# The fourth product of the first layer in two levels, over all 1024 columns at once

## The chip, the core and the metric

The kernel runs on one core of one Trainium2 chip. Its time is the device time of one execution in microseconds, 1007.34 us as the median of three runs (1006.26 to 1007.73). TensorE (PE) multiplies; each matrix product is a weight load (PEld) and a pass. VectorE (DVE), ScalarE (ACT) and GpSimd (POOL) work element by element; SyncE (SP) issues the transfers. Each engine takes its instructions strictly in the order in which the program gives them to it, and waits on semaphores for the others.

## The reference

Attention without a softmax over pairs, its heads laid side by side as 512 columns, a two-dimensional Fourier transform of that, a normalisation and two dense layers. There are 8 batches of 576 tokens, 512 columns, 2048 hidden columns, all in float32.

```
q_s = softmax(q, over head_dim);  k_s = softmax(k, over seq)
x   = q_s @ (k_s^T @ v), heads side by side            # 8 x 576 x 512
u   = x + real(fft(fft(x, over seq), over columns))
un  = (u - mean(u)) / sqrt(var(u) + 1e-6)
out = u + max(un @ w_ch1, 0) @ w_ch2                   # 512 -> 2048 -> 512
```

## The kernel before

The tokens are treated in nine groups of 512 (the last tokens of the eight batches, 64 each, make a group of their own). The first group goes through plain dense layers (`plain`), while the weights are converted and combined. The other eight, called orders 1 to 8, use a fast scheme for 2 x 2 blocks with seven products instead of eight (`strassen`). While order n is in its dense layers, the attention of batch n + 1, its transform and its normalisation are worked in between, up to order 6; order 7 has the normalisation of the last group in it, and order 8 nothing.

**First layer, `up`.** Contraction, hidden columns and tokens are each halved: 256 of 512, 1024 of 2048, 256 of 512. Four blocks j, each with a tile of 128 hidden columns from both halves, go one after the other. In a block the products go in the order 1, 6, 5, 7, 2, 4, 3 (`ORDER`), each of them two pieces of 128 hidden columns by two of contraction by 256 tokens. A float32 matrix product is two passes in the trace, so a product is 8 passes of 256 columns (L1544). The seven products share three PSUM banks: 1 and 2 in `ba`, 6, 7 and 4 in `bb`, 5 and 3 in `bc`. What stands in a bank after the first product is read out, and the next is summed on top of it. So after product 1 ACT copies `s1` out of `ba` (L1515); after 6 DVE makes `u2` = bb + s1 and after 7 `u3` = bb + s1 (L1514); block (2,2) = bc + u3 follows at once, (2,1) = bb + s1 after product 4, (1,2) = bc + u2 after product 3 (all three L1555), and (1,1) is read from `ba` after product 2 by ACT (L1551). ACT puts a ReLU on the other three (L1556). When a block is whole, `a_side` (L405 to L408) makes the four sums which the second layer needs, in orders 2 to 6 on POOL, in 7 and 8 on DVE (`e`).

**Second layer, `down`.** Order 1 uses seven products of one level, and on the way `deepen` (L1579) makes the second combinations of the second layer's weights and stores them in `w2d` (L1585). Orders 2 to 8 (`deep_down`) use two levels: product 1 as a single one (L1641), the other six in pairs, `UNITS`, with seven products of 128 x 128 pieces each (L1671), with sums made by L1617. A pair gives each of its seven steps two products, which lie in the halves of one bank.

**Streaming.** The combined weights lie in DRAM: `w1s`, for each hidden tile seven slots of 256 columns, at places `WA_AT`; `w2s`; `w2d`. Four buffers of 1 MB in SBUF form a ring; `plan` is the list of all loads, chunk after chunk, `load(n)` issues chunk n on SP (L476), and `used(n)` issues chunk n + 4 when the products of chunk n are over. `gap(i)` are four spare places of 512 columns.

**Order of the work.** It is written out by hand. Each step has a nominal time, all steps are sorted by it, and are issued in that order, which sets the order on each engine. A nominal unit stands for two of the 256-column products by pieces; in an order the first layer has 56 units (`UP`), the second 50 (`TWICE`). Times named below count from the order's start. A product's end step comes half a unit before the product's nominal end, the ReLU 0.8 after its sum, the A side 0.8 after that. The attention of the next batch has its own times: maxima, subtractions on POOL (L804), transposes on DVE (L807) and exponentials on ACT (L817, pairs one unit apart) for four sets of queries, in orders 3 and 5 from 8.5, 14, 21.5 and 27.2 on, else from 6, 13.5, 21.5 and 27.2; the subtraction comes 0.9 after the maximum, the transpose 3.5 after it, the exponentials from 4.4 to 11.4 after it. Orders 3 and 5 also have the queries that two batches share, from 5 on, with a division at 9.8 (L946 to L957) and a transpose on TensorE at 13 (L985). The key products (L755) come at 7.3 and 17.3 (order 2: three units later), the query products (L840) at 28.5 or 29.

## Time and profile before

| | us |
|---|---|
| median of three runs | 1007.34 |
| lowest, highest run | 1006.26, 1007.73 |
| span of the profiled execution | 1006.6 |
| TensorE busy (modelled) | 995.6 |
| DVE, ACT, POOL busy | 718.6, 493.2, 442.9 |
| L1544, 256-column products of the first layer, three banks | 183.3 + 123.9 + 121.5 |
| L1641 and L1671 to bank bb (second layer) | 58.3, 103.8 |

The profiled execution's own time is known by its span from the first to the last instruction; it lies 0.7 us under the median and inside the spread of the runs. A group's line in the profile has line, engine, operation, out<-in, shapes and count, then the busy time and the mean of one in ns, then the idle time before them and what ended it. In a timeline the columns are the start, the length, engine, line, operation, out<-in, shapes and count, and in brackets the idle time of the engine before. Matrix products overlap: eight passes of 256 columns read 1.89 us long and start 1.73 us apart.

### The profile page before, as it was taken

The page shows a single profiled execution, that of the slowest core. Times are in us where ns is not written, and L with a number is a line of the kernel's source. Part 1 is how long each engine was busy: PE and PEld are TensorE (multiplying, and loading weights), DVE is VectorE, ACT ScalarE, POOL GpSimd, SP SyncE. Part 2 cuts the span into 40 slices and gives each one's busy share as a digit, 9 for nine tenths or more (in the row PEclk, how much of TensorE's full clock was granted, in tenths as well). Part 3 has the DMA queues.
Part 4 walks back from the last instruction along what each step waited for, and adds up shares of the span by engine and source line. Part 5 has one row for each costly group of instructions (what it writes and reads, how often), then busy time and mean ns, then how long its engine had stood idle before and what let it go on. Part 6 is the DMA issues. An engine that isn't in the chain of part 4 may idle for free.

```text
span 1006.6 us, 19808 instructions
## 1 busy us (share of the span) xinstructions
PE 995.6 (99%) x7562; PEld 855.7 (85%) x7562; DVE 718.6 (71%) x1356; ACT 493.2 (49%) x1277; POOL 442.9 (44%) x445
## 2 busy tenths in 40 slices
PE   8999999999999999999999999999999999999998
PEld 6844464888888899889988998899889998998897
DVE  6898898666765887588756877688667945685563
ACT  4585642872468228832775177625772342151200
POOL 4263420357535637664655465655646450040000
PEclk9999999999999999999999999999999999999999
DMA  9987499687989666975677577847753765674573
GB/s 300 258 281 245 158 240 346 205 243 226 342 283 272 230 230 219 266 237 210 251 220 242 206 269 237 253 174 270 231 204 135 267 213 200 224 265 172 183 256 132
DMA packets 123559, 236.37 MB, mean 235 GB/s; under 512 B 24184, under 2 KB 88440, under 8 KB 112840
## 3 DMA queue, kind: packets, MB, share of 16 engines
q1 hardware_dynamic: 123096, 234.58, 71.0%
q8 instruction: 60, 0.98, 0.4%
q14 instruction: 35, 0.29, 0.1%
q10 hardware_dynamic: 288, 0.26, 0.1%
q0 software_dynamic: 80, 0.26, 0.1%
HBM read 199.94 MB, written 39.06 MB: 237 GB/s over the span
## 4 chain that ended last, share of the span: by engine, by line
PE 87%; DVE 7%; ACT 3%; DMA 1%; issue 1%; SPq 0%; POOL 0%; DVEq 0%; POOLq 0%
PE bb L1544 16%; PE ba L1544 11%; PE bc L1544 11%; PE bb L1671 10%; PE ba L1671 7%; PE bc L1671 7%; PE bb L1641 5%; PE bc L1479 2%; PE bb L1760 2%; PE two L840 2%; PE one L755 2%; PE two L1207 1%; PE two L1264 1%; PE ba L1479 1%; PE bc L1760 1%; PE ba L1760 1%
## 5 line engine op out<-in xcount | busy, mean ns | idle before, releaser
L1544 PE MATMUL bb<-unT,big 128*128 128x256 f32 x768 | 183.3, 380 | 0.0
L1544 PEld LDWEIGHTS bb<-unT,big 128*128 128x128 f32 x768 | 144.8, 190 | 20.7 <-DVE u L1514 0.7
L1556 ACT ACTIVATE big<-big 128x512 f32<-128x512 f32 x96 | 59.8, 629 | 147.6 <-DVE big L1555 141.0
L1544 PE MATMUL ba<-unT,big 128*128 128x256 f32 x512 | 123.9, 382 | 0.0
L1544 PE MATMUL bc<-unT,big 128*128 128x256 f32 x512 | 121.5, 380 | 0.1
L817 ACT ACTIVATE qT<-q 32x128 f32<-32x128 f32 x384 | 117.9, 307 | 5.9 <-DVE q L807 0.8
L1544 PEld LDWEIGHTS bc<-unT,big 128*128 128x128 f32 x512 | 96.9, 190 | 13.7 <-DVE big L1555 0.5
L1544 PEld LDWEIGHTS ba<-unT,big 128*128 128x128 f32 x512 | 95.5, 190 | 13.9 <-issue 0.5
L1514 DVE TENSOR_TENSOR u<-bb,s 128x512 f32<-128x512 f32 x66 | 45.2, 685 | 85.0 <-PE bb L1544 66.5
L1671 PE MATMUL bb<-big 128*128 128x128 f32 x848 | 103.8, 276 | 0.2 <-DVE u L1678 0.2
L1671 PEld LDWEIGHTS bb<-big 128*128 128x128 f32 x848 | 98.9, 192 | 1.0 <-DVE u L1678 1.0
L1390 POOL COPY unT<-unT 32x256 f32<-32x256 f32 x98 | 42.0, 428 | 90.2 <-DVE unT L1382 85.9
L1621 POOL TENSOR_TENSOR x<-x,big 128x512 f32<-128x512 f32 x45 | 60.9, 1368 | 46.0 <-DVE big L1678 19.7
L1617 DVE TENSOR_TENSOR big<-big 128x512 f32<-128x512 f32 x98 | 79.9, 842 | 0.0
L1671 PE MATMUL ba<-big 128*128 128x128 f32 x640 | 79.0, 276 | 0.0
L1671 PEld LDWEIGHTS ba<-big 128*128 128x128 f32 x640 | 75.0, 192 | 0.8
L1390 ACT COPY unT<-unT 32x256 f32<-32x256 f32 x126 | 50.7, 402 | 31.3 <-DVE unT L1382 29.5
L804 POOL TENSOR_TENSOR q<-q,qm 128x512 f32<-128x512 f32 x24 | 25.8, 1073 | 88.2 <-DVE qm L799 53.1
L405 POOL TENSOR_TENSOR big<-big 128x512 f32<-128x512 f32 x24 | 30.4, 1268 | 68.4 <-ACT big L1556 68.4
L1641 PE MATMUL bb<-big 128*128 128x256 f32 x256 | 58.3, 379 | 0.0
L1555 DVE TENSOR_TENSOR big<-bc,u 128x512 f32<-128x512 f32 x64 | 44.0, 688 | 17.3 <-PE bc L1544 16.4
L1641 PEld LDWEIGHTS bb<-big 128*128 128x128 f32 x256 | 48.0, 190 | 6.1
(336 smaller groups left out, 1917.9 us busy)
## 6 DMA issues: line engine op xcount, KB each, us to landing
big<-w2d SPq DMA_DIRECT2D x67, 1024.0 KB, 4.6
big<-w1s SPq DMA_DIRECT2D x64, 896.0 KB, 4.7
big<-w2s SPq DMA_DIRECT2D x16, 1024.0 KB, 4.8
big<-in_w_dram SPq DMA_DIRECT2D x21, 512.0 KB, 6.0
w2d<-big SPq DMA_DIRECT2D x42, 256.0 KB, 6.5
kb<-in_kT_dram SPq DMA_DIRECT2D x28, 320.0 KB, 7.8
q<-in_q_dram SPq DMA_DIRECT2D x28, 256.0 KB, 6.0
vt<-in_v_dram SPq DMA_DIRECT2D x84, 80.0 KB, 2.7
```

The source lines that it names most:

```text
L405: e1.tensor_tensor(out=to(4), in0=at(2), in1=at(3), op=ALU.add)
L817: nc.scalar.activation(to[t, i * Q:i * Q + Q], one, ACT.Exp)
L1390: copy(to, of)
L1514: plus = lambda t: V.tensor_tensor(out=temp(t), in0=box["bb"][:], in1=box["s1"][:], op=ALU.add)
L1544: nc.tensor.matmul(bank()[:, i, :], lhsT=w[:, WA_AT[m], k * P:(k + 1) * P], rhs=self.unT[g][:, B_AT[m], k, :], start=first and i == 0 and ...
L1555: steps = [(0, lambda: V.tensor_tensor(out=hp(i), in0=bank()[:], in1=u()[:], op=ALU.add)), (0.8, lambda: nc.scalar.activation(hp(i), hp(i) ...
L1556: (0.8, lambda: nc.scalar.activation(hp(i), hp(i), ACT.Relu))]
L1617: e.tensor_tensor(out=to(o), in0=to(x), in1=to(y), op=op)
L1621: E.tensor_tensor(out=x, in0=x, in1=tile(m), op=ALU.add)
L1641: nc.tensor.matmul(box[name][:, i, :], lhsT=h[p][:, A_AT[m], i * P:(i + 1) * P], rhs=self.stream[n][:, p, :], start=p == 0 and (m != 1 or ...
L1671: nc.tensor.matmul(box[place[n]][:, i, :], lhsT=own(m)(A_AT[n])[:, f, :], rhs=w[:, r // 2, r % 2 * P:r % 2 * P + P], start=first and f == ...
L1760: nc.tensor.matmul(bank()[:, i, :], lhsT=h[p][:, A_AT[m], i * P:(i + 1) * P], rhs=w[:, p, :], start=first and i == 0 and p == 0, stop=p == ...
```

## The change

In orders 2 to 8 the fourth product leaves the four blocks of the first layer (`REST`), and is made once for all four, with a second level of the same scheme: its 256 x 1024 x 256 is halved in each direction, and seven products of four pieces of 128 x 128 by 128 tokens remain. This is `deep_up`, put between block 0 and block 1.

- Its weights' second combinations are made once, in order 1 at the start of the second layer (`deepen_up`): eight loads of slot `WA_AT[4]` into a buffer of the ring, two sums on DVE, two on POOL, seven stores to the new `w1d`. Slot 4 of `w1s` is now the last one, so that later loads take six slots.
- In each later order four of the seven weight sets come as a chunk of the ring, after the two chunks of block 0; the three others come by `weights` into `gap(1)` to `gap(3)`, at nominal 3.
- DVE makes four differences of 128 x 128 of the tokens (`minus`, nominal 8.0 to 8.9), into `gap(0)`. The seven products use the banks `ba`, `bb`, `bc` as before, 1.02 units apart, with a copy to `s1`, `u2`, `u3`, three more sums on DVE and one copy on ACT; the results go to slot `A_AT[5]` of the four blocks.
- In the blocks, `there` writes bb + s1 after product 7 straight to the place of (2,1), and (2,2) is made from it. `late` adds the deep result to (2,1), on `e` (POOL in orders 2 to 6, DVE in 7 and 8), and a ReLU follows. For block 0 that and the A side wait for the deep product: late add at 20.2, A side at 22.0.
- A first layer has now 4 x 12 + 7.2 = 55.2 units (`DEEP_UP`, `ups`).

```diff
-WA_AT = {1: 0, 2: 1, 3: 6, 4: 2, 5: 4, 6: 5, 7: 3}
+WA_AT = {1: 0, 2: 1, 3: 5, 4: 6, 5: 3, 6: 4, 7: 2}
+REST = tuple(m for m in ORDER if m != 4)
+DEEP_UP = 7.2
...
+        self.w1d = d.tile([P, len(ORDER), GT], F32, tag="w1d", name="w1d", bufs=1)
+        self.plan, self.at_up, self.at_down, self.at_deep = [], {}, {}, {}
         for at in range(1, B + 1):
-            self.base[at] = len(self.plan)
-            self.plan += [self.w1s[p][:].rearrange("p a n -> p (a n)") for pair in PAIRS for p in pair]
+            slots = len(ORDER) - (at > 1)
+            self.at_up[at] = []
+            for j, pair in enumerate(PAIRS):
+                for p in pair:
+                    self.at_up[at].append(len(self.plan))
+                    self.plan.append(self.w1s[p][:, 0:slots].rearrange("p a n -> p (a n)"))
+                if at > 1 and j == 0:
+                    self.at_deep[at] = len(self.plan)
+                    self.plan.append(self.w1d[:, 0:4].rearrange("p a n -> p (a n)"))
+            if at == 1:
+                self.at_deep[at] = len(self.plan)
+                self.plan.append([self.w1s[p][:, WA_AT[4]] for i in range(2) for p in [pair[i] for pair in PAIRS]])
+            self.at_down[at] = len(self.plan)
...
-    def strassen(self, product, step, out, early=lambda *a: []):
+    def strassen(self, product, step, out, early=lambda *a: [], u3=None):
...
+        if u3:
+            there = lambda: V.tensor_tensor(out=u3, in0=box["bb"][:], in1=box["s1"][:], op=ALU.add)
+            ends[7] = [(0, there)] + at(0.8, out[2, 2](get("bc"), lambda: u3) + out[2, 1](None, None))
...
-        for m in ORDER:
+        for m in REST if u3 else ORDER:
...
-                    if i == 2:
+                    if i == 2 and not wait:
                         steps.append((1.6, lambda: self.a_side(hp, hp, e, e)))
...
+            def late(t, hp=hp, relu=relu):
+                return [(t, lambda: e.tensor_tensor(out=hp(1), in0=hp(1), in1=hp(4), op=ALU.add)), (t + 1.6, lambda: relu(1))]
+
+            out = {(1, 1): c11, (2, 2): other(3), (1, 2): other(2)}
+            out[2, 1] = other(1) if not deep else lambda *_, j=j, late=late: late(1.6) if j else []
+            steps += at(t, self.strassen(product, 1, out, u3=hp(1) if deep else None))
+            t += 2 * len(REST if deep else ORDER)
+            waits = (-0.5, 2 if deep and j == 0 else 4.5 if j < NP // 2 - 1 else -0.5)
+            steps += [(t + dt, lambda n=n: self.used(n)) for dt, n in zip(waits, n)]
+            if deep and j == 0:
+                steps += at(t, self.deep_up(order, g))
+                t += DEEP_UP
+                steps += late(t + 1) + [(t + 2.8, lambda hp=hp: self.a_side(hp, hp, e, e))]
...
+    def deep_up(self, order, g):
...
+        place = {1: "ba", 2: "ba", 6: "bb", 7: "bb", 4: "bb", 5: "bc", 3: "bc"}
...
+        to = lambda i: self.hblock(A_AT[5], i % 2, 1 - i // 2)
...
+        def weights():
+            for i in range(3):
+                nc.sync.dma_start(self.gap(1 + i).rearrange("p j n -> p (j n)"), self.w1d[:, 4 + i, :])
...
+        def product(k):
...
+            for j in range(4):
+                w = self.stream[n][:, 2 * k + j // 2, j % 2 * P:j % 2 * P + P] if k < 4 else self.gap(k - 3)[:, j, :]
+                nc.tensor.matmul(box[name][:, j, :], lhsT=w, rhs=b_at(B_AT[m]), start=first and j == 0, stop=True,
+                                 skip_group_check=True)
+            if k == 3:
+                self.used(n)
...
+        def ends(m):
+            if m == 1:
+                nc.scalar.copy(temp("s1"), box["ba"][:])
+            if m == 6:
+                plus(temp("u2"), "bb", "s1")
+            if m == 7:
+                plus(temp("u3"), "bb", "s1")
+                plus(to(3), "bc", "u3")
+            if m == 2:
+                nc.scalar.copy(to(0), box["ba"][:])
+            if m == 4:
+                plus(to(2), "bb", "s1")
+            if m == 3:
+                plus(to(1), "bc", "u2")
+
+        steps = [(-9, weights)]
+        for i, (o, x, y) in enumerate(((4, 1, 0), (1, 3, 1), (5, 3, 4), (6, 2, 5))):
+            steps.append((-4 + 0.3 * i, lambda o=o, x=x, y=y: minus(o, x, y)))
+        for k, m in enumerate(ORDER):
+            steps += [(1.02 * k, lambda k=k: product(k)), (1.02 * k + 0.9, lambda m=m: ends(m))]
+        return steps
+
+    def deepen_up(self):
...
+        return [(0, lambda: make(V, 4, 2, 3, ALU.add)), (1, lambda: make(V, 2, 0, 2)), (1, lambda: make(G, 5, 4, 0)),
+                (2.5, lambda: make(G, 6, 1, 5)), (0, lambda: keep(raw)), (6, lambda: keep([m for m in ORDER if m not in raw])),
+                (7, lambda: self.used(n))]
```

More of the change, by code (lines that the diff above doesn't have):

```diff
@@ L439, in combine @@
             engines, times = (nc.vector,) * 4, (0, 0.4, 0.8, 1.2)
-            to, first, second = self.w1s[p][:], slice(0, 2), slice(2, 3)
+            to, first, second, third = self.w1s[p][:], slice(0, 2), slice(6, 7), 2
             one, two = halves(w[:, p, :]), quarter(3).unsqueeze(1)
@@ L475, in load @@
         w = self.big[:, k * NP * HD:(k + 1) * NP * HD]
-        self.nc.sync.dma_start(w[:, :self.plan[n].shape[1]], self.plan[n])
+        some = self.plan[n] if isinstance(self.plan[n], list) else [self.plan[n]]
+        end = 0
+        for of in some:
+            end += of.shape[1]
+            self.nc.sync.dma_start(w[:, end - of.shape[1]:end], of)
         self.stream[n] = w.rearrange("p (a n) -> p a n", n=HD)
@@ L1534, in up, with product @@
         nc, V = self.nc, self.nc.vector
-        steps = []
-        base, e = self.base[order], V if order >= B - 1 else nc.gpsimd
+        steps, t = [], 0
+        deep, e = order > 1, V if order >= B - 1 else nc.gpsimd
         for j in range(NP // 2):
             hp = lambda i, h=self.hpairs(j, 2): h[:, :, i, :]
-            def product(m, bank, first, j=j):
+            n = self.at_up[order][2 * j:2 * j + 2]
+            def product(m, bank, first, n=n):
                 def run(i):
-                    w = self.stream[base + 2 * j + i]
+                    w = self.stream[n[i]]
                     for k in range(2):
@@ L1862, in timed, with ups @@
         return steps + at(t + 24 + 1.65 * soon, blk.norm(groups[b]))
+    def ups(order):
+        return UP if order == 1 else 2 * len(REST) * (NP // 2) + DEEP_UP
     fetch, convert = blk.weights()
```

57 lines of the change are left out of this document (42 added, 15 removed).

## The prediction

> **What bounds the kernel now.** I read the page first, then stretches of one order each, then the timeline engine by engine around the first layer of orders 3, 4 and 8. The page (span; busy share; granted clock by slices; chain):
>
> ```profile
> span 1006.6 us, 19808 instructions
> PE 995.6 (99%) x7562; PEld 855.7 (85%) x7562; DVE 718.6 (71%) x1356; ACT 493.2 (49%) x1277; POOL 442.9 (44%) x445
> PEclk9999999999999999999999999999999999999999
> PE 87%; DVE 7%; ACT 3%; DMA 1%; issue 1%; SPq 0%; POOL 0%; DVEq 0%; POOLq 0%
> ```
>
> Order 4 by stretches: length, then busy time (instructions) of PE, weight load, DVE, ACT, POOL, clock, DMA share, GB/s:
>
> ```profile
> 496.60:602.70 106.10, 106.10 (x921) 97.76 (x921) 77.34 (x146) 58.92 (x163) 60.96 (x59) 1.00 0.71 232
> ```
>
> TensorE is never without work, and its clock is full. So each microsecond of TensorE that the change saves comes off the end, and each wait it adds goes on. The reader is to see that today nothing waits: the slack between dependent products is what the change spends. The profiled span, 1006.6, lies 0.7 below the median of the runs, 1007.34; I add my sum to the median.
>
> **What the products cost.** Timeline of order 4, first the 256-column products of L1544 (8 passes each), then the 128-column ones of the second layer (16 passes each):
>
> ```profile
> 516.94 1.89 PE L1544 MATMUL bb<-unT,big 128*128 128x256 f32 x8
> ...
> 523.85 1.03 PE L1544 MATMUL ba<-unT,big 128*128 128x256 f32 x4
> ...
> 469.84 1.95 PE L1671 MATMUL bc<-big,unT 128*128 128x128 f32 x16
> ...
> 480.56 1.95 PE L1671 MATMUL bb<-big 128*128 128x128 f32 x16
> ```
>
> Four products lie from 516.94 to 523.85: 1.73 us each. Six pieces lie from 469.84 to 480.56: 1.787 each, 0.112 a pass. Removed in an order: the fourth product of four blocks, 4 x 1.73 = 6.91 us. Added: seven products of 8 narrow passes, 56 x 0.112 = 6.25, or 0.89 each. Gain 0.66 an order, 4.6 over orders 2 to 8. That is all the change can win, and only without waits.
>
> **What an add costs TensorE.** Order 8, where the other engines have little else to do (PE, DVE, ACT), and two rows of order 7:
>
> ```profile
> 913.55 1.89 PE L1544 MATMUL bb<-unT,big 128*128 128x256 f32 x8
> 915.28 1.89 PE L1544 MATMUL ba<-unT,big 128*128 128x256 f32 x8
> 915.48 0.69 DVE L1514 TENSOR_TENSOR u<-bb,s 128x512 f32<-128x512 f32 x1 [0.78 <-PE bb L1544]
> 916.20 0.69 DVE L1555 TENSOR_TENSOR big<-bc,u 128x512 f32<-128x512 f32 x1
> 920.46 1.89 PE L1544 MATMUL ba<-unT,big 128*128 128x256 f32 x8
> 920.66 0.69 DVE L1555 TENSOR_TENSOR big<-bc,u 128x512 f32<-128x512 f32 x1 [1.03 <-PE bc L1544]
> 921.38 0.63 ACT L1556 ACTIVATE big<-big 128x512 f32<-128x512 f32 x1 [1.10 <-DVE big L1555]
> 922.44 0.59 ACT L1515 COPY s<-ba 128x512 f32<-128x512 f32 x1 [0.43 <-PE ba L1544]
> ...
> 831.58 0.68 DVE L1514 TENSOR_TENSOR u<-bb,s 128x512 f32<-128x512 f32 x1
> 832.32 1.99 PE L1544 MATMUL bb<-unT,big 128*128 128x256 f32 x8
> ```
>
> An add starts 0.20 after the next product and lasts 0.69; in order 7 an add ends at 832.26 and the waiting product starts at 832.32, 0.06 later. So a bank is free 0.95 after its product's end; with a second add behind (916.20 + 0.69, against 915.28) after 1.67.
>
> Ordinary blocks: the fourth product separated the seventh from the third, which reuses bank bc after u3 and (2,2). Now only the second does, 1.73 against 1.67: it fits by 0.06 when DVE is idle. In the first block of orders 7 and 8 one of the new differences (nominal 8.0) stands between the two adds. The small 128x128 form takes 0.28 (row below): 1.67 + 0.28 - 1.73 = 0.22 late. In the first block of the earlier orders an attention batch lies there and covers it.
>
> **The deep product, orders 7 and 8.** Its first product is copied to s1 by ACT, but the last ReLU of block 0 (12.3) is queued before that copy (12.9). Counting from the end of block 0 (920.46 stands for it): ReLU 921.38 to 922.01, copy to 922.62, u2 to 923.35, seventh product at 923.40 instead of 920.46 + 3 x 0.89 = 923.14. That is 0.26 late, and the fourth, which needs u3 out of bb, 0.05. Gain there: 0.66 - 0.31 - 0.22 = 0.13 an order.
>
> **The deep product, orders 2, 4, 6.** ACT is shared with the exponentials of the next batch (L817), pair by pair at one nominal unit. DVE, ACT and POOL of order 4:
>
> ```profile
> 506.79 1.89 PE L1544 MATMUL bb<-unT,big 128*128 128x256 f32 x8
> 508.52 1.89 PE L1544 MATMUL bc<-unT,big 128*128 128x256 f32 x8
> 507.55 1.25 ACT L817 ACTIVATE qT<-q 32x128 f32<-32x128 f32 x4
> 512.03 1.26 ACT L817 ACTIVATE qT<-q 32x128 f32<-32x128 f32 x4
> 513.31 0.59 ACT L1515 COPY s<-ba 128x512 f32<-128x512 f32 x1
> 511.81 1.04 POOL L804 TENSOR_TENSOR q<-q,qm 128x512 f32<-128x512 f32 x1 [3.56 <-DVE qm L799]
> 512.81 1.27 POOL L405 TENSOR_TENSOR big<-big 128x512 f32<-128x512 f32 x1
> 516.74 1.27 POOL L408 TENSOR_TENSOR big<-big 128x512 f32<-128x512 f32 x1
> 521.30 0.71 DVE L807 STREAM_TRANSPOSE q<-q 128x512 f32<-128x512 f32 x1 [0.56 <-POOL q L804]
> ```
>
> The third product moves to 506.79, the deep one starts at 508.52. Its copy stands behind the ReLU (509.44 to 510.07) and the pair of nominal 12.4 (0.63): 510.70 to 511.29. Then u2 to 512.02 and the seventh at 512.08, due at 511.20: 0.88 late, plus 0.05.
>
> **Orders 3 and 5** have the shared queries as well, and DVE is the later one. Order 3:
>
> ```profile
> 399.62 0.69 DVE L1555 TENSOR_TENSOR big<-bc,u 128x512 f32<-128x512 f32 x1
> 404.16 0.68 DVE L1555 TENSOR_TENSOR big<-bb,s 128x512 f32<-128x512 f32 x1
> 401.45 1.89 PE L1544 MATMUL bb<-unT,big 128*128 128x256 f32 x8
> 403.17 1.89 PE L1544 MATMUL bc<-unT,big 128*128 128x256 f32 x8
> 404.90 0.60 PE L985 MATMUL one<-ident,q 128*128 128x128 f32 x4
> 230.47 0.28 DVE L1129 TENSOR_TENSOR eo<-eo 128x128 f32<-128x128 f32 x1
> ```
>
> From 400.31 to 404.16 DVE serves attention, 3.85 us, then the add of the fourth product. In the new order the same work, with four differences of 0.28, stands before the add that frees bc: it ends at 405.98. The deep fifth product wants bc at 404.96. Behind it ReLU, copy and u2 follow (0.63, 0.59, 0.69 with releases): the seventh at 408.02, due at 406.29 with the transposes of L985 (0.44) counted. That is 1.73 late, plus 0.05.
>
> **The A side of block 0, orders 2 to 6.** Today POOL makes it at nominal 15.1, behind one subtraction of the queries (L804) and clear of the next (22.4). The change moves it to 22.0, behind the late add (20.2, 1.27 on POOL). Counted from the end of the deep product: last add to 0.89, late add to 2.2, four sums (512.81 to 518.01: 5.2) to 7.4, L804 to 8.45. The transpose L807 (nominal 25), which waited 0.56 at 521.30, now holds DVE until then and ends at 9.2. Behind it stand `there` (0.69), a maximum of the queries (0.68) and (2,2): 11.2. The third product of block 1 wants bc at 5 x 1.73 = 8.64 plus an attention batch of 1.8 (524.80 to 526.60 in the next fence, order 4): 10.44. So 0.75 late. The fence also has a stretch of order 1 and L1617 in two stretches, 350 to 388 and 960 to 1000 us, for what follows.
>
> ```profile
> 524.80 1.16 PE L840 MATMUL two<-pairs,qT 64*64 64x65 f32 x64
> ...
> 526.60 1.13 PE L1544 MATMUL ba<-unT,big 128*128 128x256 f32 x4
> 245.00:258.00 13.00, 13.00 (x71) 11.72 (x70) 8.39 (x21) 2.03 (x3) 4.94 (x5) 1.00 1.05 347
> L1617 DVE TENSOR_TENSOR big<-big 128x512 f32<-128x512 f32 x11 | 10.3, 962 | 0.0
> L1617 DVE TENSOR_TENSOR big<-big 128x512 f32<-128x512 f32 x10 | 6.4, 683 | 0.0
> ```
>
> **At nothing.** DVE gives up four adds (2.8 us) and gets five and four differences (4.6) an order, ACT two copies (1.2), POOL four late adds (5.1): beside TensorE, apart from the places above; without that cover the sum is 8 us an order. A late add also delays a ReLU and the sums for the second layer's units, which have the single product (L1641) and attention in front. Streaming: each of eight loads shrinks by 128 KB, 1 MB of kept weights and three loads of 256 KB come in, 0.75 MB more. The SP queue passes three more issues and one load in an order whose DMA share is 0.71. The ring's wait at the deep chunk is for the fourth deep product, well ahead.
>
> **Order 1's second layer.** deepen_up adds eight loads (1 MB) and seven stores (1.75 MB), four 128x512 sums and a held ring slot. The SP queue and the DMA engines are full there (245 to 258: share 1.05, 347 GB/s). Low end 0, since it only adds work and TensorE has weights ahead; high end 2.75 MB / 347 GB/s = 7.9 us. I take 0: TensorE is busy for all of that stretch, and the seventh product's weights are wanted some 25 us later.
>
> [...] L1617, two SBUF inputs, takes 962 ns beside POOL (350 to 388) and 683 without (960 to 1000): 0.28 an instruction. [...] The adds that free banks read PSUM and one SBUF tensor, so I book none of it.
>
> **Sum.** Orders 2, 4, 6: 0.66 - 0.93 - 0.75 = -1.0 each, -3.1. Orders 3, 5: 0.66 - 1.78 - 0.75 = -1.9 each, -3.7. Orders 7, 8: +0.3. Together 6.5 us slower: 1007.3 + 6.5 = 1013.8. The waits booked add up to 11.1 us (6.5 + 4.6): with half of them the kernel is 1 us slower, and with half as much again elsewhere (16.7 less 4.6) 12 us slower.
>
> **Rivals.** (1) Faster: the waits don't form, because queries and ReLUs drift ahead of TensorE while it waits once and later waits vanish. For: the copies of orders 7 and 8 start at once. Against: the queues are in order, and L817 already pushes the copy to 513.31 in order 4. Gain 4.6 less 0.1 an order: 1003.4. It decides when the waits of orders 2 to 6 stay below 0.73 us an order. (2) Cancelling at about that point: 1007.3. (3) The transfers of order 1 are not hidden: 1013.8 + 7.9 = 1021.7; for it the share of 1.05, against it that TensorE has none of the waits today. [...]
>
> **How the numbers follow.** Forecast 0.58, (1) 0.24, (2) 0.06, (3) 0.06, (4) 0.06. Two runs of this kernel differ by about 0.1%, so 0.2% is what can be told from no change. Faster 0.24, same 0.06, slower 0.70. The range goes from 1004 into (1) to 1021; the forecast's own is 1008.5 to 1020.
>
> **What would show it.** Right: in orders 2 to 6 TensorE idles before the seventh deep product (copy to s1 late) and before the third product of block 1 (DVE behind L807 behind POOL); orders 7 and 8 a little shorter; passes of 0.112. Wrong: in orders 2 to 6 TensorE goes through the deep product and block 1 in its own time (6.25 us, then 1.73 a product), or it waits for a load of weights in order 1 or 2.

## The result, and the profile after

The changed kernel takes 1066.4 us, the median of four runs (1065.0 to 1068.8), against 1006.9 for the kernel before beside it: a ratio of 1.059 (95% interval 1.058 to 1.061). It is 59.5 us slower. The prediction had said 1013.8, with a range from 1004 to 1021: the sign was right, the size was not.

The page of the changed kernel (span, busy shares, the chain that ended last):

```profile
span 1063.2 us, 20359 instructions
...
PE 1007.0 (95%) x7730; PEld 860.2 (81%) x7730; DVE 759.5 (71%) x1401; ACT 499.6 (47%) x1291; POOL 469.3 (44%) x467
...
PE 61%; DVE 23%; DMA 5%; ACT 4%; issue 3%; POOL 3%; SPq 1%; POOLq 0%; DVEq 0%; ACTq 0%
```

TensorE was the chain to 87% and is now 61%; DVE went from 7% to 23%. DVE's busy time rose by 41 us (718.6 to 759.5), while the sums that the change adds to it come to some 20 us at their undisturbed durations: 12.6 by the prediction's count (seven orders of 4.6 - 2.8), eight late adds of 0.69 in orders 7 and 8, and two sums of 0.7 in order 1. The rest is, on balance, instructions that became longer. The transform's thirty differences of 128 x 128 (L1129 before, L1147 after), which the change leaves as they are, went from 8.5 to 25.0 us.

Where the time lies is seen by cutting the trace at the first product of each first layer (L1544 before, L1566 after). Length of orders 1 to 7 in us (order 8 has no end of that kind; its time to the end of the span is 98.2 before and 98.3 after):

| order | 1 | 2 | 3 | 4 | 5 | 6 | 7 |
|---|---|---|---|---|---|---|---|
| before | 110.0 | 106.5 | 105.3 | 106.0 | 105.4 | 107.0 | 93.3 |
| after | 112.3 | 121.4 | 114.5 | 117.0 | 114.6 | 118.4 | 93.4 |
| more | 2.3 | 14.9 | 9.2 | 11.0 | 9.3 | 11.4 | 0.1 |

Orders 2 to 6 lose 55.8 us, order 1 loses 2.3, orders 7 and 8, with no attention in them, are as long as they were. Order 4 by stretches (length, then busy time of PE, weight load, DVE, ACT, POOL; clock; DMA share; GB/s), to be read beside the row of order 4 in the prediction:

```profile
521.40:638.40 117.00, 108.61 (x944) 99.08 (x943) 84.08 (x151) 59.99 (x165) 65.67 (x63) 0.99 0.69 218
```

In the kernel before, the view of TensorE's waits has no row at all for orders 2 to 6 (284 to 815 us). In the changed kernel the same view (tile and line that waited, engine and line that released it: us in total, times, longest), from 285 to 872 us:

```profile
PE two L1225 <- DVE eo L1148: 13.2, 5, 2.7
PE bb L1566 <- DVE u L1532: 11.3, 7, 2.1
PE bc L1566 <- DVE big L1580: 10.4, 9, 2.5
PE bb L1629 <- DVE u L1640: 5.1, 3, 2.2
PE ba L1566 <- POOL unT L1408: 2.2, 1, 2.2
PE one L1003 <- DVE q L975: 1.6, 2, 0.8
PE bc L1566 <- DVE x L1890: 0.8, 1, 0.8
PE two L858 <- DVE F L1043: 0.7, 1, 0.7
```

These are 45.3 us of idle time. Counted from the start of one product to the start of the next, the wait at 538.67 below comes to 2.34 us where its idle time is 2.18; where the text says how late a product is, it is by the starts. The deep product itself (L1629) has 5.1 of the 45.3. The largest, 13.2, is a wait of the transform (L1225), which the change doesn't touch; the next two, 21.7 together, are ordinary blocks (L1566) that wait for `u2` and for the sums that free `bc`. The longer waits of order 4 in the timeline (start, length, engine, line, out<-in, count; in brackets the idle time before):

```profile
538.67 1.16 PE L1629 MATMUL bb<-big 128*128 128x128 f32 x8 [2.18 <-DVE u L1640]
...
564.43 3.68 PE L1566 MATMUL bb<-unT,big 128*128 128x256 f32 x8 [2.11 <-DVE u L1532]
567.94 1.89 PE L1566 MATMUL ba<-unT,big 128*128 128x256 f32 x8
...
593.14 1.22 PE L1225 MATMUL two<-ft,eo 128*128 128x144 f32 x8 [2.65 <-DVE eo L1148]
```

The product at 564.43 waits for `u2`, and `u2` for the copy to `s1`. The block's first product starts at 556.98 and is over by 558.9, but its copy stands behind exponentials on ACT until 563.07:

```profile
561.15 1.89 ACT L835 ACTIVATE qT<-q 32x128 f32<-32x128 f32 x6
563.07 0.58 ACT L1533 COPY s<-ba 128x512 f32<-128x512 f32 x1
563.68 0.69 DVE L1532 TENSOR_TENSOR u<-bb,s 128x512 f32<-128x512 f32 x1 [4.18 <-ACT s L1533]
```

Five of the seven waits for `u2`, 9.1 of the 11.3 us, are of this kind; one of 1.8 in order 5 stands behind sums of the attention on DVE.

The product at 564.43 takes 3.51 us to the start of the next instead of 1.73. The stretch around it shows why (clock is the last number but two):

```profile
564.20:568.00 3.80, 3.57 (x9) 2.88 (x10) 3.77 (x4) 3.64 (x13) 3.72 (x3) 0.55 0.21 39
```

After the wait of 2.1 us TensorE had a clock of 0.50 for 3.4 us (564.5 to 567.9). There are four such stretches in the trace, all of 3.4 us at 0.50 (from 335.8, 359.7, 564.5 and 796.6 us), each behind one of the longer waits (2.48, 2.58, 2.11 and 2.13 us). By an estimate from their length, half of 3.4, each costs another 1.7 us or so, about 7 us in all. Waits of that length are not always followed by one: four of the five before L1225 (2.65 to 2.66 us) were not.

### The profile page after: what moved, and what is told of

Its sections match the earlier page's. It is cut to its first block, busy times and chain, and to the rows that moved or that the text cites. A ratio compares the mean times of both kernels' runs of the same rounds, so it can differ in the third digit from the quotient of the medians.

```text
span 1063.2 us, 20359 instructions
## 1 busy us (share of the span) xinstructions
PE 1007.0 (95%) x7730; PEld 860.2 (81%) x7730; DVE 759.5 (71%) x1401; ACT 499.6 (47%) x1291; POOL 469.3 (44%) x467
## 4 chain that ended last, share of the span: by engine, by line
PE 61%; DVE 23%; DMA 5%; ACT 4%; issue 3%; POOL 3%; SPq 1%; POOLq 0%; DVEq 0%; ACTq 0%
PE bb L1786 10%; PE bc L1566 7%; PE ba L1786 6%; PE bc L1786 6%; PE bb L1566 6%; PE ba L1566 6%; PE bb L1756 3%; DMA w2d<-big 2%; PE bc L1497 2%; DVE eo L1147 2%; PE bb L1629 2%; DVE big L1580 2%; DVE eo L1148 2%; PE ba L1497 1%; PE bb L1497 1%
## 5 line engine op out<-in xcount | busy, mean ns | idle before, releaser
L1566 PE MATMUL bb<-unT,big 128*128 128x256 f32 x544 | 133.6, 388 | 11.3 <-DVE u L1532 11.3
L1566 PE MATMUL bc<-unT,big 128*128 128x256 f32 x512 | 124.9, 387 | 11.3 <-DVE big L1580 10.4
L1566 PEld LDWEIGHTS bb<-unT,big 128*128 128x128 f32 x544 | 103.6, 193 | 29.6 <-DVE u L1532 14.8
L1566 PE MATMUL ba<-unT,big 128*128 128x256 f32 x512 | 122.8, 382 | 2.2 <-POOL unT L1408 2.2
L1566 PEld LDWEIGHTS bc<-unT,big 128*128 128x128 f32 x512 | 95.9, 191 | 29.8 <-DVE big L1580 16.3
L1566 PEld LDWEIGHTS ba<-unT,big 128*128 128x128 f32 x512 | 95.9, 191 | 16.4 <-POOL unT L1408 2.6
L1732 DVE TENSOR_TENSOR big<-big 128x512 f32<-128x512 f32 x98 | 75.6, 799 | 0.0
L1532 DVE TENSOR_TENSOR u<-bb,s 128x512 f32<-128x512 f32 x38 | 26.0, 685 | 42.0 <-ACT s L1533 20.8
L1793 DVE TENSOR_TENSOR u<-bb,s 128x256 f32<-128x256 f32 x40 | 16.8, 421 | 51.0 <-PE bb L1786 48.3
```

Of the source, the lines that this page charges most:

```text
L1532: plus = lambda t: V.tensor_tensor(out=temp(t), in0=box["bb"][:], in1=box["s1"][:], op=ALU.add)
L1566: nc.tensor.matmul(bank()[:, i, :], lhsT=w[:, WA_AT[m], k * P:(k + 1) * P], rhs=self.unT[g][:, B_AT[m], k, :], start=first and i == 0 and ...
L1732: e.tensor_tensor(out=to(o), in0=to(x), in1=to(y), op=op)
```

## The experiments

Two theories stood at the start. One was the prediction's: the late parts of the deep product (its copy on ACT, the late A side of block 0) make the waits. The rival was that POOL and DVE hinder each other. Neither held the greater part, and a third, formed after the first runs, was that blocks of six products stand in another place against the attention's fixed nominal times, and have lost the time that the fourth product gave to ACT and DVE. All times are medians, all ratios are to the kernel before, run beside each.

**One wait at a time.** Four kernels take one suspect each out of the changed kernel.

All of block 0 to 3's POOL work to DVE:

```diff
-        deep, e = order > 1, V if order >= B - 1 else nc.gpsimd
+        deep, e = order > 1, V if order > 1 else nc.gpsimd
```

> Late adds and all A sides of the first layer on DVE in orders 2 to 6 (nothing of the first layer left on POOL); order 1 as before. Theory A (the waits come from POOL: its A sides stand before the queries' subtractions, and its reads of SBUF stretch DVE's adds with two SBUF inputs from 0.28 to 1.3 us): the waits before the transform (2.8 us an order) and in blocks 1 and 2 (about 5 us an order) go, some come from DVE's 14 us more an order; about 1035. Theory B (the slack between dependent products is spent, and DVE is simply too busy): DVE has still more to do, so 1070 to 1090.

1056.3 us, ratio 1.048 (1.043 to 1.052). The wait of the transform is gone; in its place TensorE waits for `u2` behind the A sides, which now stand on DVE:

```profile
PE bb L1566 <- DVE u L1532: 26.3, 15, 3.5
```

A resource was freed and a queue lengthened: 10 us gained of 59.

The A side of block 0 behind the queries' subtraction:

```diff
-                steps += late(t + 1) + [(t + 2.8, lambda hp=hp: self.a_side(hp, hp, e, e))]
+                steps += late(t + 1) + [(t + 3.4, lambda hp=hp: self.a_side(hp, hp, e, e))]
```

> Only the A side of block 0 moves from nominal 22.0 to 22.6, behind the subtraction of the third queries (22.4) in POOL's queue. Theory A1 (that subtraction held the transpose on DVE, and that the exponentials, so that block 1 and the copy to s1 of block 2 were late): the 0.7 us of block 1 and the 2.3 us of block 2, with the half clock after it (1.8), go in orders 3 to 6 and much of 4.9 us in order 2; about 1046. Theory A2 (ScalarE is overloaded there anyway): within 3 us of 1066.4.

1064.2 us, 1.058 (1.056 to 1.060). Block 1's wait for (2,2), 0.7 in orders 4 and 6 and 0.9 in order 3, goes, as the prediction's mechanism has it. Block 2's product that needs `u2` stays 2.3 late in orders 2, 4 and 6 and is still 1.0 late in orders 3 and 5 (1.6 and 1.4 before the move): that the same subtraction held block 2 is true for a small part only.

The last block's A side on DVE, behind the transform's sums:

```diff
-                        steps.append((1.6, lambda: self.a_side(hp, hp, e, e)))
+                        far = deep and hp is last
+                        steps.append((2.9 if far else 1.6, lambda: self.a_side(hp, hp, *((V, V) if far else (e, e)))))
```

> Only the A side of the last block goes to DVE in orders 2 to 6, behind the transform's last sums (nominal 58.1 instead of 56.3). Theory A (these four sums on POOL stretch the transform's sums on DVE to 1.3 us each and so hold TensorE for 2.8 us in every one of five orders): 5 x 2.8 and the half clock after them, 1066.4 - 14 to -19 = about 1050. Rival (the transform is late because its inputs are): the wait stays, within 3 us of 1066.4.

1049.4 us, 1.043 (1.041 to 1.044). All five waits of L1225 are gone, and 17 us with them: the 13.2 of the waits, and a mean clock of 0.995 in the profiled execution against 0.993. What made this wait is seen on DVE and POOL in the changed kernel's order 4:

```profile
585.36 0.28 DVE L1147 TENSOR_TENSOR eo<-eo 128x128 f32<-128x128 f32 x1
...
585.89 0.68 DVE L1580 TENSOR_TENSOR big<-bc,u 128x512 f32<-128x512 f32 x1
...
587.69 1.35 DVE L1147 TENSOR_TENSOR eo<-eo 128x128 f32<-128x128 f32 x1
589.08 1.31 DVE L1148 TENSOR_TENSOR eo<-eo 128x128 f32<-128x128 f32 x1
590.31 1.35 DVE L1147 TENSOR_TENSOR eo<-eo 128x128 f32<-128x128 f32 x1
591.69 1.30 DVE L1148 TENSOR_TENSOR eo<-eo 128x128 f32<-128x128 f32 x1
...
587.37 1.52 POOL L419 TENSOR_TENSOR big<-big 128x512 f32<-128x512 f32 x1 [2.41 <-ACT big L1576]
588.97 1.26 POOL L420 TENSOR_TENSOR big<-big 128x512 f32<-128x512 f32 x1
590.19 1.31 POOL L421 TENSOR_TENSOR big<-big 128x512 f32<-128x512 f32 x1
591.58 1.26 POOL L422 TENSOR_TENSOR big<-big 128x512 f32<-128x512 f32 x1
```

A sum of 128 x 128 with both inputs in SBUF takes 0.28 us at 585.36, where POOL has nothing to do, and 1.30 to 1.35 in the four rows beside POOL's sums, where each ends 0.15 to 0.16 us after one of POOL's. Four such sums come to 5.3 us instead of 1.1. The kernel before has the same A side at the same place, but there only two of the last four of these sums were slowed by it, and TensorE had its product in time:

```profile
552.71 0.28 DVE L1129 TENSOR_TENSOR eo<-eo 128x128 f32<-128x128 f32 x1
553.03 1.33 DVE L1130 TENSOR_TENSOR eo<-eo 128x128 f32<-128x128 f32 x1
554.28 0.28 DVE L1129 TENSOR_TENSOR eo<-eo 128x128 f32<-128x128 f32 x1
554.59 1.25 DVE L1130 TENSOR_TENSOR eo<-eo 128x128 f32<-128x128 f32 x1
```

(The sum at 554.28 took 0.28 in the midst of POOL's sums: not every one is slowed.) In the changed kernel a first layer is 0.8 units shorter, so one more sum of the second layer (L1732) stands before the last four of the transform, and all four fall beside the A side.

The copy to `s1` in the deep product from ACT to DVE:

```diff
-                nc.scalar.copy(temp("s1"), box["ba"][:])
+                V.tensor_copy(temp("s1"), box["ba"][:])
```

> Only the deep product's copy to s1 goes from ScalarE to DVE in orders 2 to 8. My theory of the prediction (it stands behind a ReLU and exponentials in ScalarE's queue): 0.9 us in order 2, 2.35 in orders 4 and 6, about 0.3 in 7 and 8, and half clock of some 2: about 1058. Rival (the late thing is the sum u2 on DVE): within 2 us of 1066.4.

1065.4 us, 1.057 (1.056 to 1.059). The seventh deep product is 0.79 late in orders 4 and 6 instead of 2.34, so ACT's queue was the cause of two thirds of that; in order 2 it is 0.82 instead of 0.91, so there it was not. The time hardly moves: the clock is 0.96, 0.97 and 0.99 in orders 2, 4 and 6, against 0.97, 0.99 and 0.99 in the changed kernel (mean 0.990 against 0.993). That is one execution of each; two of the changed kernel's own four had 0.990.

Three of these moves together (A side of block 0 later, last A side on DVE, `s1` on DVE):

> The three moves together: A side of block 0 behind the queries, A side of the last block on DVE, deep copy to s1 on DVE. If the waits are independent: 1066.4 - 2.2 - 17.0 - 1.1 = 1046. If TensorE only meets the next late thing (theory C): 1046 to 1050; if they held each other: below 1040.

1041.2 us, 1.035 (1.032 to 1.038). Together they gain 25 us, 5 more than one by one (17.0, 2.2 and 1.0), though one of the four runs took 1047.3; 34 us are still there. Another set, with every A side on DVE and 3 units later (block 0: 1.8), and the `s1` copy on DVE; one of its edits:

```diff
-                        steps.append((1.6, lambda: self.a_side(hp, hp, e, e)))
+                        steps.append((4.6 if deep else 1.6, lambda: self.a_side(hp, hp, e, e)))
```

> As the first-layer-on-DVE kernel, and besides each A side stands 3 units later (block 0: 1.8), behind the next block's u2, and the deep copy to s1 is on DVE. In that kernel u2 waited 2.1 to 3.6 us three times an order behind A sides. Theory A (order in DVE's queue decides, not its load): these waits go, 1056.3 - 5 x 6 = about 1025. Rival (DVE is full): 1045 or more.

1050.5 us, 1.042 (1.039 to 1.044). It moves the waits to the sums that free `bc` (14.1 us) and to `u2` (10.3) and is no better than the single move of the last A side.

**Is it the moved A side alone?** The kernel before, with block 0's A side 7.2 units later in orders 2 to 6 and nothing else:

```diff
-                        steps.append((1.6, lambda: self.a_side(hp, hp, e, e)))
+                        steps.append((1.6 + 7.2 * (j == 0 and 1 < order < B - 1), lambda: self.a_side(hp, hp, e, e)))
```

> The kernel before, with one thing of the change: in orders 2 to 6 the A side of block 0 stands 7.2 units later (nominal 22.3), ahead of the subtraction of the third queries in POOL's queue. Theory A (that order alone holds DVE's transpose, and with it the adds that free banks): with the fourth product's slack of 1.7 us still there, 0 to 1 us an order, 1007 to 1012. Rival (A sides and transform's sums collide at every place, so any move costs): 1015 or more.

1007.3 us, 1.000 (1.000 to 1.001). A late A side costs nothing where the fourth product is still there and every other step has its old place.

**What order 1 costs.** The deep product in orders 7 and 8 alone, with all of order 1's work (the main lines):

```diff
-        deep, e = order > 1, V if order >= B - 1 else nc.gpsimd
+        deep, e = order >= B - 1, V if order >= B - 1 else nc.gpsimd
...
-        return UP if order == 1 else 2 * len(REST) * (NP // 2) + DEEP_UP
+        return UP if order < B - 1 else 2 * len(REST) * (NP // 2) + DEEP_UP
```

> The second level only in orders 7 and 8; orders 2 to 6 make the fourth product in the blocks as before; order 1 still makes and stores the second combinations. Theory A (order 1 costs little, orders 7 and 8 nothing, all else comes from the deep product among the attention): 1007.0 + 2.3 for order 1 + 0.2 = 1009.5. Rival (order 1's extra transfers and sums put order 2 late, which lost 14.9 us): 1015 or more.

1012.6 us, 1.006 (1.004 to 1.007). Order 1 is 2.5 us longer and order 2 another 2.0, though neither has the deep product; orders 3 to 6 are as before, order 7 is 93.4 as in the full change. The waits of orders 2 to 6 (285 to 818 us) are three, all at the start of order 2:

```profile
PE ba L1566 <- POOL unT L1408: 2.4, 1, 2.4
PE bc L1566 <- DVE x L1890: 0.8, 1, 0.8
PE bb L1566 <- DVE u L1532: 0.4, 1, 0.4
```

The first product of order 2 waits for the normalised tokens of its group. The same without the deep product anywhere, and with the sums of order 1 but none of its stores:

```diff
-                (2.5, lambda: make(G, 6, 1, 5)), (0, lambda: keep(raw)), (6, lambda: keep([m for m in ORDER if m not in raw])),
-                (7, lambda: self.used(n))]
+                (2.5, lambda: make(G, 6, 1, 5)), (7, lambda: self.used(n))]
```

> No deep product in any order; order 1 loads the fourth weights and makes their four sums as in the changed kernel, but stores nothing. The kernel with the stores and the deep product in orders 7 and 8 alone took 1012.6, 4.5 us of it in orders 1 and 2. If the 1.75 MB of stores are the cause (DVE waited 7.7 us for a store there): about 1007.5. If it is the sums and the ring slot: 1011 or more.

1010.0 us (nine runs, 1006.5 to 1012.3), 1.003 (1.001 to 1.004). Order 1 has its old length, order 2 is 1.4 longer. That lies between the two forecasts, so the stores carry about half of order 1's price, and the loads and sums the rest. How they hold up POOL's part of the tokens was not tried. The trace shows one step of it: in order 1 a sum on DVE stands 7.7 us until a store of `w2d` has landed, against 0.9 in the kernel before and 5.1 without the new stores.

**The blocks of six without the deep product.** Here the fourth product is left out altogether, once with blocks of 12 nominal units and once with the gap left open, so that every other instruction keeps its place. The first of them does not have the places of the change: without the deep product's 7.2 units, blocks 1 to 3 start 2, 4 and 6 units earlier than in the kernel before, and not later. The last part of `strassen` in the second of them:

```diff
-        for m in REST if u3 else ORDER:
+        for m in ORDER:
+            if u3 and m == 4:
+                t += 2 * step
+                continue
```

> The blocks of orders 2 to 8 make six products and the fourth is left out altogether: no deep product, no late adds, (2,1) without its last term; order 1 as in the changed kernel. TensorE has 7 x 6.91 = 48.4 us less than before. Theory A (the waits come from the deep product, the late adds and the moved A side): 1007.0 - 48.4 + 2.3 = 961, and some 3 more. Rival (the fourth product was the slack between dependent products, so six-product blocks themselves wait): 5 us an order more, 985 or more.

> The kernel with six products only (the fourth left out altogether, no late adds, (2,1) without its last term), but with the nominal times of the kernel before: a gap of two units where the fourth product stood, so that every other instruction keeps its place in its engine's queue. With six products and shifted times it took 1023.6. Theory C1 (shifted places in the queues): 1007 - 48.4 + 6 = about 965. Theory C2 (the attention's own chain through DVE, ACT and POOL takes an order's time, and TensorE's fourth product only filled it): orders 2 to 6 stay near 105 us, about 1000.

With shifted times 1023.6 us, 1.016 (1.015 to 1.018); in the old order 984.5 us, 0.977 (0.976 to 0.979). Both make the same products, and TensorE has 48.4 us less to do than before in each. A shift of places in the queues, here to earlier ones, is alone worth 39 us. And even in the old order 22.5 us are gained and not 48.4: orders 7 and 8 gain all of their 6.9 us or nearly, orders 2 to 6 only 1.4 to 4.1. Their waits (286 to 804 us) name what the missing product had covered:

```profile
PE ba L1566 <- ACT big L1573: 8.4, 5, 1.9
PE ba L1566 <- POOL unT L1405: 2.9, 1, 2.9
PE bc L1566 <- DVE big L1580: 2.2, 5, 1.0
...
```

`ba` holds product 2 until ACT has made (1,1) of it, and the next block's first product wants it back. Two products lay between; now one does.

**More work for TensorE.** The changed kernel with one more product in each block (the seventh's weights once more, nobody reads it), and blocks of 14 units again, with the attention's nominal times as they were:

```diff
+            ends[4] = []
...
-        for m in REST if u3 else ORDER:
+        for m in ORDER:
...
-                        nc.tensor.matmul(bank()[:, i, :], lhsT=w[:, WA_AT[m], k * P:(k + 1) * P],
+                        nc.tensor.matmul(bank()[:, i, :], lhsT=w[:, WA_AT[7 if deep and m == 4 else m], k * P:(k + 1) * P],
...
-            t += 2 * len(REST if deep else ORDER)
+            t += 2 * len(ORDER)
```

> The changed kernel, and in each block of orders 2 to 8 an eighth-pass filler stands where the fourth product stood (the weights of the seventh once more, its result unused), with the nominal times of the blocks as before. TensorE has 7 x 6.91 = 48.4 us more to do than in the changed kernel: 1066.4 + 48.4 = 1115 if the waits are of the deep product's making. Theory C (the fourth product was the slack of the blocks, and without it the blocks wait about as long): the waits of blocks 1 to 3 (some 5 us an order) go, 1090 or less; 1007 + 7 x 6.3 + 6 for order 1 = 1057 if all go.

1080.7 us, 1.072 (1.071 to 1.074). 48.4 us more work (28 x 1.73) cost 14.3 us. The waits before L1225 and for the sums that free `bc` are gone; those for `u2` are not (285 to 880 us):

```profile
PE bb L1567 <- DVE u L1532: 9.4, 6, 1.9
```

But this edit changes two things. It puts the product back, and it moves places again: blocks 1 to 3 and the second layer now start 7.2 units later than in the kernel before, against 5.2, 3.2, 1.2 and -0.8 in the change. So the 34 us of waits that it saves (48.4 - 14.3) can't be put down to the slack alone.

**The deep product in the old order.** The last question was whether the loss is the deep product's own, or that of the shifted places. Two kernels keep the deep product and give all else its old place in its queue: the blocks keep 14 units, the attention from nominal 14 on moves by 7.2.

```diff
-                steps += late(t + 1) + [(t + 2.8, lambda hp=hp: self.a_side(hp, hp, e, e))]
+                steps += late(t + 1) + [(t + 1.2, lambda hp=hp: self.a_side(hp, hp, e, e))]
...
-        if b + 1 < B:
-            steps += at(t, blk.ahead(b + 1))
-        steps += at(t, blk.attention_timed(b, start, end)) + at(t + end, blk.folded(b))
+        others = blk.attention_timed(b, start, end) + at(end, blk.folded(b))
+        if b + 1 < B:
+            others = blk.ahead(b + 1) + others
+        steps += [(t + dt + DEEP_UP * (order > 1 and dt >= 14), step) for dt, step in others]
```

> The deep product of the change stays as it is, but in orders 2 to 6 the blocks keep the nominal 14 units that they had with seven products (the place of the fourth is left empty), the attention's and the next batch's steps from nominal 14 on move 7.2 units back, and the A side of block 0 comes right behind the late add. So every instruction that the change does not touch keeps its place in its queue against the blocks, as before the change. Theory 1 (the loss is the shift of the blocks against the attention in the in-order queues, and the lost slack): the run with the same order and no fourth product at all took 984.5 us, with order 1 at 3 more than before; the deep product adds 7 x 6.25 = 43.8 and its own waits of at most 1 us an order: 1028 to 1036 us. Theory 2 (the loss is the deep product's own: its copy, its adds, its late adds on POOL): at least 1050 us, with the waits behind the deep product and block 1 as in the change.

> As the last run, and in the place of the fourth product each block of orders 2 to 8 makes one more product with the seventh's weights, whose result nobody reads: TensorE has 28 x 1.73 = 48.4 us more, and the slack between the seventh and the third product is back. Theory 1: nearly all waits go, since the order of the queues and the slack are both those of before the change; what is left is the kernel before, plus the deep products (43.8 us), plus order 1 and 2 (4.5 us): 1055 to 1062 us, 20 us below the filler in the change's own order (1080.7). Theory 2: the waits of the deep product stay, 1070 us or more.

1056.1 us, 1.048 (1.045 to 1.050), and 1074.9, 1.067 (1.065 to 1.069): by the numbers, theory 2. But the edit had put block 0's A side ahead of the ReLU of its (2,1) part, so that the second layer was fed another value there, and ACT stood still at that ReLU until POOL had read the part (order 3 of the first of the two, ACT):

```profile
432.30 0.63 ACT L1579 ACTIVATE big<-big 128x512 f32<-128x512 f32 x1 [5.93 <-POOL big L422]
```

Both were made again with the A side 1.6 units later (`t + 2.8`, as in the change), behind the ReLU.

> In the run before, block 0's A side was made ahead of the ReLU of its (2,1) part, and that ReLU (ACT) then waits until POOL has read the part. Here the A side comes behind the ReLU (1.6 units later); all else is as there. Theory 1 (the earlier run lost most of its time to that mistake, and the shifted places are the main cause of the change's loss): 1028 to 1040 us. Theory 2 (the deep product's own instructions on ACT, DVE and POOL delay the first parts of block 1, whatever the places of the attention): 1050 to 1060 us, with waits of c11's ReLU in block 1 that stay within 1 us of those of the earlier run.

> The filler in the fourth product's place, in the old order, with the A side of block 0 behind the ReLU of its (2,1) part. This is the kernel before with a deep product set in and the fourth product's result not read. Theory 1: 1055 (1007 + 7 x 6.25 + 4.5 of order 1 and 2) to 1063 us. Theory 2: 1070 to 1077 us, as the earlier run with the filler (1074.9): the excess over 1055 is what the deep product itself disturbs.

1035.6 us, 1.028 (1.026 to 1.030), and 1060.8, 1.053 (1.051 to 1.054): theory 1, both within its ranges. One step in the wrong place had cost 20 us and turned the verdict round. The waits of TensorE, first of the kernel without the filler (286 to 842 us), then with it (285 to 854):

```profile
PE ba L1569 <- ACT big L1576: 8.2, 5, 1.8
PE bb L1632 <- DVE u L1643: 5.5, 5, 1.8
PE ba L1569 <- POOL unT L1408: 2.4, 1, 2.4
PE one L1003 <- DVE q L975: 2.1, 2, 1.1
PE bc L1569 <- DVE big L1583: 2.0, 5, 1.0
```

```profile
PE bb L1630 <- DVE u L1641: 2.6, 2, 1.3
PE ba L1567 <- POOL unT L1408: 1.9, 1, 1.9
PE bc L1567 <- DVE x L1891: 0.8, 1, 0.8
PE bb L1567 <- DVE u L1532: 0.4, 1, 0.4
```

With the slack and the old places, what is left of the waits is the start of order 2 and the deep product in orders 3 and 5. Without the slack (1,1) is late in every order; ACT of order 4 in the first of the two shows sixteen exponentials in front of it:

```profile
549.28 5.11 ACT L835 ACTIVATE qT<-q 32x128 f32<-32x128 f32 x16
554.41 0.63 ACT L1579 ACTIVATE big<-big 128x512 f32<-128x512 f32 x1
555.07 0.60 ACT L1576 ACTIVATE big<-ba 128x512 f32<-128x512 f32 x1
```

Put together from these runs: the shifted places cost 30.9 us (1066.4 - 1035.6), the waits before L1225 and for `u2` among them. The lost slack costs 23.2 (1035.6 + 48.4 - 1060.8), and the rest is 9.4 (1060.8 - 48.4, against 1007.6 less the 4.6 that the narrow products save). These make 63.5 of the 64.1 between the kernel after and the kernel before less its saving.

Of the 23.2, the two views of waits account for 14.5 (20.2 without the filler, 5.7 with it); where the others go was not traced. The 9.4 can be laid out by orders, with the filler against the kernel before plus 6.25 us for the deep product: 2.1 in order 1, 2.0 in order 2, 1.7 each in orders 3 and 5, 0.4 each in orders 4 and 6, 0.5 each in orders 7 and 8. How places and slack share the 54 us depends on which is restored first: with the filler in both, the attention's places are worth 19.9 (1080.7 - 1060.8), for a larger shift than that of the change. The slack alone, in the change's own places, was not run.

That DVE is simply too busy, the rival in several of these expectations, is settled too: in order 4 it is busy for 83.8 us with the filler and the old places, as in the changed kernel (84.1), and TensorE has no row of waits there.

No kernel that makes the deep product in all orders came under the kernel before. It saves 4.6 us of TensorE in all, and its work in order 1 alone costs as much (4.5 us by the lengths of orders 1 and 2).

## Why the prediction was wrong, step by step

- **What bounds the kernel, and the saving: right.** The narrow products start 0.89 us apart where nothing is late, as booked. Orders 7 and 8 were booked 0.13 shorter each and are 0.1 longer each: in order 7 the deep product takes 6.71 us (881.89 to 888.60), where 6.25 and 0.31 of waits were booked.
- **"Ordinary blocks ... it fits by 0.06 when DVE is idle": this is the step that failed.** It looked at bank `bc` alone and with an idle DVE, and then booked no wait for ordinary blocks in orders in which DVE is not idle (the row of order 4 in the prediction has it busy 77 of 106 us). In orders 2 to 6 these blocks wait 21.7 us, 10.4 at `bc` and 11.3 at `bb`. With the old places, and the fourth product still missing, `bb` no longer waits, `bc` waits 2.0, and `ba`, which the step left out, waits 8.2 for (1,1); with the filler these two are gone as well. So the slack of the fourth product was that of `ba` and `bc`, and the waits at `bb` come from the next point. The prediction's own finding, that TensorE never waits, says that other engines were always in time; by how much was worked out at two places and assumed elsewhere.
- **The places in the queues: not a step at all.** Block 1 starts at nominal 19.2 instead of 14, block 2 at 31.2 instead of 28, block 3 at 43.2 instead of 42, while the attention keeps its times. The prediction followed the steps that the change moves past others, and only round the deep product. But blocks 1 to 3 were all moved past the attention's steps on ACT, DVE and POOL, and the second layer came 0.8 units earlier. Giving them their old places back is worth 31 us, more than the whole range of the forecast.
- **The deep product in orders 2, 4, 6, 0.88 + 0.05 late: right in kind, short in size.** The copy to `s1` does stand behind exponentials, and the seventh product waits for it, but it is 2.34 us late in orders 4 and 6. In order 2 it is 0.91 late, as booked, but by luck: with the copy on DVE it is still 0.82. In orders 4 and 6 three of the four differences on DVE fell beside POOL's sums of the second layer and took 0.76 to 1.24 instead of 0.28, and the transposes and exponentials behind them came later:

```profile
529.15 4.03 POOL L1736 TENSOR_TENSOR x<-x,big 128x512 f32<-128x512 f32 x3
529.54 1.02 DVE L1619 TENSOR_TENSOR big<-unT 128x128 f32<-128x128 f32 x1
531.76 1.56 DVE L1619 TENSOR_TENSOR big<-unT,big 128x128 f32<-128x128 f32 x2
534.74 1.27 ACT L835 ACTIVATE qT<-q 32x128 f32<-32x128 f32 x4 [2.35 <-DVE q L825]
537.31 0.58 ACT L1644 COPY s<-ba 128x512 f32<-128x512 f32 x1
```

- **Orders 3 and 5, 1.78 late at the deep product: too much there.** The deep product is 0.96 late, at the transposes L1003 between its passes, and not for the seventh.
- **The A side of block 0, 0.75: right in size and place** (0.70 in orders 4 and 6, 0.93 in order 3), and the run that moves it shows the cause. It is 0.7 of the 11 us that each of orders 4 and 6 loses.
- **Order 1 at 0: wrong.** 4.5 us by the lengths of orders 1 and 2 in the run that has the deep product in orders 7 and 8 alone. The bounds 0 to 7.9 held it; the rival that priced it looked for TensorE waiting on weights, and it waits for tokens.
- **"The adds that free banks read PSUM and one SBUF tensor, so I book none of it": the second step that failed.** A sum with both inputs in SBUF went from 0.28 to 1.35 us beside POOL's (585.36 and 587.69 above). The adds that free banks are indeed not stretched: all 169 adds of L1532, L1539, L1580 and L1640 in the changed kernel, each of 128 x 512 out of a bank, took 0.65 to 0.69 us, 0.69 also at 563.68, in the midst of POOL's sums of block 1 (561.39 to 566.88). But they and TensorE stand behind those that are. Booking none of it missed the 13.2 us before L1225, and 0.28 an instruction, the difference of two means over sums of which some are stretched and some not (L1617 to `big` in the trace before: 0.65 to 1.77 us), was no bound. The trace before had a row of 1.33 for a sum of 0.28; the prediction quoted the 0.28.
- **The half clock after a wait: not foreseen.** The trace before has a mean clock of 1.000, so no row could price it. Four stretches cost about 7 us, by the estimate above.

## What to carry to other kernels

A product that is dropped takes its time away from every engine that worked under it: before booking a saving on the bound engine, go through each bank or buffer that it stood between, and ask which engine, with which queue in front of it, must now be ready one product sooner. In a program with an order written out by hand, a step that makes one part longer and another shorter moves all later steps of one kind past those of another; give the other steps the same shift first, and measure that alone. And when an experiment's edit moves a step, look at what that step now reads or blocks before the verdict is believed: here one misplaced step hid 20 us.

## What the runs showed of the hardware that had not been expected

- A wait of 2.1 us on TensorE was followed by 3.4 us at a clock of 0.50 (564.5 to 567.9), so by the estimate of 1.7 us the price of that wait is near 4 us and not 2; four of the five waits of 2.58 to 2.66 us before L1225 were not followed by it.
- Beside POOL sums of 1.26 to 1.52 us, with both inputs of each in SBUF, a DVE sum of 0.28 us took 1.30 to 1.35 (587.69 to 592.99, four in a row): the small instruction was as long there as the large one beside it. One of the four at the same place in the kernel before got through in 0.28.
- With the old places, 48.4 us of useless products cost 25.2 us (1060.8 - 1035.6): under waits of this kind about half of TensorE's work was free.
